# Two token blocks share an accumulator by halves: four 64x64 parts of TensorE in the last loop of an attention and spectral-mixing kernel

## The chip, the cores and the metric

One core of a Trainium2 chip runs the whole program. The metric is the device time of one execution in microseconds (us). A ratio is the mean time of one kernel's fast runs over that of the other's of the same rounds, with a 95% interval; so it is not quite the ratio of the medians that stand beside it. The span of a trace is some 1.8 us shorter than the time. In profile lines PE is TensorE, DVE VectorE, ACT ScalarE, POOL GpSimd and SP SyncE; PSUM is the memory that TensorE's accumulators lie in.

## The reference, cut to what matters

Causal attention over 8 batches, 8 heads and 576 positions gives x (8, 576, 512). The second half mixes it:

```python
def _moe_ref(x, w_r, w_i, w_ch):
    X = np.fft.rfft(x, axis=1)
    ... # 64 modes, each multiplied by its own complex 512x512 matrix
    y = np.fft.irfft(Y, n=S, axis=1)
    u = x + y
    return (u + np.maximum(u @ w_ch, 0.0)).astype(np.float32)
```

576 positions are four full blocks of 128 and one of 64 per batch.

## The kernel before: the parts that matter

The last loop makes the output. A pair is two token blocks, (b, T) and (b, T+1); for the 64-row tails a pair packs four of them. Each pair has two accumulators `us` for u = x + y and two, `zs`, for u @ w_ch. The product x @ w_ch of a pair was made earlier and kept, in one of two ways: as two fp16 digits, which TensorE adds back with four identity matmuls ("e"), or as fp32, which ACT copies into PSUM ("s").

```python
ways = dict(zip(kept, "esesessesesseses"))

def keep_product(i, xx, z):
    if ways[i] != "e":
        nc.scalar.copy(out=z1s[i][:, xx], in_=z)
        return
    nc.scalar.copy(out=z1s[i][:, 0, xx], in_=z)               # high digit
    nc.vector.tensor_tensor(out=z1s[i][:, 1, xx], in0=z,      # low digit
                            in1=z1s[i][:, 0, xx], op=ALU.subtract)

def start_u(i):                      # x into u: one full matmul for each block
    ...
            nc.tensor.matmul(us[i][x][r, :]..., ident, x_all[: r.stop - r.start, :, bb, T, :],
                             start=True, stop=False, ..., tile_position=(0, r.start))

def finish(i):
    for x, (b, T) in enumerate(pairs[i]):
        o = rs[i][:, x, :]
        ...
        nc.vector.tensor_tensor(out=o, in0=us[i][x], in1=o, op=ALU.add)
        for r, bb, _ in parts(b, T):
            nc.sync.dma_start(out=out[bb, bass.ds(T * P, r.stop - r.start), :], in_=rs[i][r, x, :])

for i in range(NPRE, len(pairs)):
    pre(i)                           # digits of z ("e"), then y into z: two matmuls
    start_u(i)
    add_y(us[i], i, 0)               # y into u: two matmuls
    if ways.get(i + 1) == "s":
        seed(i + 1)                  # ACT copy
    ...
    relu(i, 2 if i == last else 1)   # ACT
    finish(i)                        # two additions on DVE, two stores from SyncE
```

Ahead of the loop, a stretch bound by the transfer of weights multiplies the modes and keeps the remaining products (`late`, the pairs not kept during attention), the last pair's last.

The softmax here doesn't subtract the row's maximum and nothing guards it: scores larger than these inputs give would overflow.

## Time and profile before

| what | before |
|---|---|
| median of three runs | 459.39 us |
| last group of weights multiplied, in the trace | 418.11 us |
| last loop on PE | 423.90 to 452.1 us |
| a store of 256 KB: form, time to landing | 128 rows in one run, 2.0 to 4.5 us (medians 2.3 and 2.6) |

### The profile page before, as it was taken

The numbers are of one execution on the slowest core, as the hardware profiler recorded it, in microseconds if no ns is written. First come the engines' busy times: TensorE is split into PE (matmuls) and PEld (weight loads), VectorE is DVE, ScalarE is ACT, GpSimd is POOL, SyncE is SP. The second block draws the span as 40 slices with busy tenths as digits, with TensorE's granted clock in tenths as the row PEclk, the third lists the DMA queues.
The fourth block names the chain that finished last, engine by engine and source line by source line (L and its number), as shares of the span: only waits on it lengthen the run. The fifth ranks groups of instructions, "written<-read, shape, count | busy, mean of one in ns | idle before, by whom it ended". The sixth has DMA issues, their size and how long they took to land.

```text
span 457.1 us, 10262 instructions
## 1 busy us (share of the span) xinstructions
PE 339.1 (74%) x4177; PEld 217.2 (48%) x4209; DVE 237.3 (52%) x528; ACT 219.1 (48%) x382; POOL 182.9 (40%) x269
## 2 busy tenths in 40 slices
PE   1779968966562979936587766779967769797995
PEld 1556646644341656614355544446643326343432
DVE  7777645653242556624345544466656425442675
ACT  1587856554241747723445345446622220221895
POOL 6755555544345555344454444355423223200000
PEclk9999999998586889957778799899999778999999
DMA  9999999999999999999999999999999999995688
GB/s 177 201 203 203 202 201 204 202 204 204 204 204 201 202 202 202 204 205 204 199 192 205 204 204 204 204 203 202 207 206 212 210 210 210 214 214 105 235 285 319
DMA packets 109375, 94.54 MB, mean 207 GB/s; under 512 B 28480, under 2 KB 104512, under 8 KB 109328
## 3 DMA queue, kind: packets, MB, share of 16 engines
q0 software_dynamic: 98960, 81.81, 113.0%
q1 hardware_dynamic: 10368, 12.07, 8.5%
q8 instruction: 33, 0.54, 0.4%
q14 instruction: 14, 0.11, 0.1%
HBM read 164.56 MB, written 9.44 MB: 381 GB/s over the span
## 4 chain that ended last, share of the span: by engine, by line
DMA 70%; PE 20%; issue 4%; POOL 3%; DVE 2%; DVEq 0%; POOLq 0%
DMA w_sb<-in_moe_w_i_dram 44%; DMA q<-in_q_dram 13%; DMA w_sb<-in_moe_w_r_dram 5%; PE yp L441 3%; PE sc_ps L365 3%; PE av_ps L394 2%; DMA x_all<-in_moe_w_r_dram 2%; DMA k<-in_k_dram 2%; PE sc_ps L359 2%; DMA y_acc<-in_moe_w_i_dram 2%; PE tr_ps L324 2%; DMA y_acc<-in_moe_w_r_dram 2%; PE u_ps L694 2%; PE z_ps L675 2%; PE u_ps L675 2%
## 5 line engine op out<-in xcount | busy, mean ns | idle before, releaser
L373 ACT ACTIVATE p_sb<-sc_ps,cumt_sb 128x576 f16<-128x576 f32 (+1 forms) x256 | 141.9, 636 | 45.8 <-PE sc_ps L365 45.4
L217 POOL DMA_DIRECT2D w_sb<-in_moe_w_i_dram x60 | 45.1, 751 | 81.7 <-PE yp L441 36.8
L217 POOL DMA_DIRECT2D w_sb<-in_moe_w_r_dram x60 | 45.4, 757 | 65.2 <-DMA w_sb<-in_moe_w_r_dram 26.1
L217 POOL DMA_DIRECT2D v<-in_v_dram x72 | 50.8, 707 | 31.3 <-DMA w_sb<-in_moe_w_r_dram 8.4
L324 PE MATMUL tr_ps<-ident,q 64*64 64x64 bf16 x576 | 17.1, 208 | 55.4 <-DMA q<-in_q_dram 55.4
L359 PE MATMUL sc_ps<-negm,ident 128*128 128x256 bf16 x256 | 55.0, 300 | 0.3
L441 PE MATMUL yp<-w_sb,xs 128*32 128x512 bf16 x480 | 37.0, 408 | 22.2 <-DMA w_sb<-in_moe_w_i_dram 18.1
L327 DVE COPY qtA<-tr_ps 64x576 bf16<-64x576 bf16 x32 | 23.8, 743 | 50.8 <-PE tr_ps L324 50.7
L344 ACT ACTIVATE p<-sc_ps,cumt 128x64 f16<-128x64 f32 x32 | 10.1, 314 | 74.2 <-PE sc_ps L340 74.2
L394 PE MATMUL av_ps<-v,p_sb 128*128 128x65 f16 x1024 | 43.7, 196 | 0.0
L394 PEld LDWEIGHTS <-p_sb 128*128 128x128 f16 x1024 | 38.9, 99 | 4.8 <-issue 0.7
L327 DVE COPY ktA<-tr_ps 64x576 bf16<-64x576 bf16 x32 | 24.0, 750 | 32.7 <-PE tr_ps L324 32.7
L324 PEld LDWEIGHTS <-q 64*64 64x64 bf16 x576 | 13.3, 120 | 58.0 <-DMA q<-in_q_dram 56.9
L441 PEld LDWEIGHTS <-xs 128*32 128x32 bf16 x512 | 22.9, 169 | 32.3 <-issue 28.8
L365 PE MATMUL sc_ps<-qtB,ktB 128*128 128x64 bf16 (+2 forms) x160 | 34.8, 322 | 3.7 <-issue 2.4
L365 PE MATMUL sc_ps<-qtA,ktA 65*128 65x512 bf16 (+2 forms) x192 | 36.1, 297 | 0.3 <-DVE ktA L327 0.3
L399 DVE TENSOR_REDUCE den<-av_ps 128x5 f32<-128x10 f32 x64 | 10.8, 169 | 46.4 <-PE av_ps L394 46.4
L404 DVE TENSOR_TENSOR x_all<-av_ps,rcp 128x320 f16<-128x320 f32 x64 | 31.5, 492 | 2.2
L327 ACT COPY ktB<-tr_ps 64x576 bf16<-64x576 bf16 x32 | 20.3, 634 | 19.7 <-DVE ktA L327 18.8
L365 PEld LDWEIGHTS <-ktB 128*128 128x128 bf16 x192 | 22.4, 117 | 14.8 <-issue 6.3
L324 PE MATMUL tr_ps<-ident,k 64*64 64x64 bf16 x576 | 17.5, 210 | 14.0 <-DVE qtB L327 10.5
L601 PE MATMUL z_ps<-wch_sb,xs 128*128 128x512 f16 x96 | 26.2, 423 | 0.8 <-DVE xs L595 0.8
(112 smaller groups left out, 526.4 us busy)
## 6 DMA issues: line engine op xcount, KB each, us to landing
w_sb<-in_moe_w_r_dram POOLq DMA_DIRECT2D x60, 512.0 KB, 11.9
w_sb<-in_moe_w_i_dram POOLq DMA_DIRECT2D x60, 512.0 KB, 11.9
q<-in_q_dram POOLq DMA_DIRECT2D x32, 144.0 KB, 9.7
k<-in_k_dram POOLq DMA_DIRECT2D x32, 144.0 KB, 10.1
v<-in_v_dram POOLq DMA_DIRECT2D x72, 64.0 KB, 9.7
out_dram<-r_sb SPq DMA_DIRECT2D x16, 256.0 KB, 2.3
out_dram<-r_w SPq DMA_DIRECT2D x16, 256.0 KB, 2.6
x_all<-in_moe_w_i_dram POOLq DMA_DIRECT2D x3, 512.0 KB, 10.0
```

Of the source, the lines that this page charges most:

```text
L217: nc.gpsimd.dma_start(out=dst, in_=src)
L324: nc.tensor.transpose(ps[rows, r, :], src[rows, r, :], ident16[rows, rows])
L327: copy(out=dst[n % NQ][rows, :].rearrange("d (p r) -> d p r", r=R), in_=ps[rows].rearrange("d r p -> d p r"),)
L359: nc.tensor.matmul(ps[:, bass.ds(w * S, W)], ident16, negm[:, bass.ts(r, W)], start=True, stop=False, skip_group_check=True,)
L365: nc.tensor.matmul(ps[:, c0 : c0 + i1 - i0], keys[:, w, r, :], qt[:, i0:i1], start=False, stop=True, skip_group_check=True,)
L373: nc.scalar.activation(out=pt[:, poff[x] : poff[x] + S - w * W], in_=ps[:, w * S : (w + 1) * S - w * W], func=ACTF.Exp, bias=cumt_sb[:, x, ...
L394: nc.tensor.matmul(ps[:, I, r : r + NCH], lhsT, rhs, start=(i == 0), stop=(i == len(todo) - 1), skip_group_check=True,)
L399: nc.vector.tensor_reduce(out=den, in_=ps[:, :, 0 : VW : NCH], axis=mybir.AxisListType.X, op=ALU.add)
L404: nc.vector.tensor_tensor(out=x_all[:, g, b, :, D * h : D * h + D], in0=ps[:, :, 1 : NCH], in1=rcp.unsqueeze(2).to_broadcast([P, NT, D]), ...
L441: nc.tensor.matmul(ps[32 * cg : 32 * cg + 32, :], cols[:, c0 : c0 + 32, c * MC + 2 * cg + par], wt[(g, c, ri, par)][:, cg, :], start=(x == ...
L601: nc.tensor.matmul(z[:, x, :], xts[i][:, x, dt, :], wch_sb[:, dt, :], start=(dt == 0), stop=(last and dt == DT - 1), skip_group_check=True,)
L675: nc.tensor.matmul(dst[x][r, :], G_sb[rows, bass.ds(T * P, r.stop - r.start)], yv[rows, bb, which, :], start=start, stop=True, skip_group_ ...
```

## The change

Its intent: TensorE is the bound of the last loop, and an identity matmul uses a 128x128 array to move 128 rows. If accumulator h holds half h (64 rows) of both blocks of a pair, four 64x64 parts can bring four quarters in at once. The columns of the constant that brings y in are permuted to match, and for ACT pairs the copies of transposed x are too (not shown). The letters change to twelve digit pairs ("f") and four ACT pairs, and the output rows of an accumulator are now two runs of 64 rows.

```diff
+    two = np.arange(NF * P).reshape(NF // 2, 2, 2, HP).transpose(0, 2, 1, 3).reshape(-1)
+    G_np[:, : NF * P] = G_np[:, two]
-    ways = dict(zip(kept, "esesessesesseses"))
+    ways = dict(zip(kept, "ffsfffffsfsffsff"))
 ...
     def start_u(i):
+        if halved(i):
+            for h in range(2):
+                for x, (b, T) in enumerate(pairs[i]):
+                    own = slice(HP * h, HP * (h + 1))
+                    nc.tensor.matmul(
+                        us[i][h][HP * x : HP * (x + 1), :].rearrange("p (g d) -> p g d", d=P),
+                        ident16h[own, own], x_all[own, :, b, T, :],
+                        start=True, stop=False, ..., tile_position=(HP * h, HP * x),
+                    )
+            return
 ...
     def finish(i):
+            if halved(i):
+                two = out[b, bass.ds((T - x) * P, 2 * P), :]
+                nc.sync.dma_start(out=two.rearrange("(x h p) e -> h x p e", x=2, h=2)[x], in_=o)
+                continue
 ...
-                        zs[i][:, x, :], ident16h, z1s[i][:, y, x, :],     # four full matmuls
+                            zs[i][HP * x : HP * (x + 1), h, :], ident16h[own, own],
+                            z1s[i][own, y, x, :],                        # eight of 64x64
```

## The prediction

> **What bounds the kernel now.** I read four views, in this order. First the page's slices, to see which stage is bound by what: DMA is at nine tenths in every slice until the weights are in, PE at nine only in some. Second the chain of waits, backwards from the end: up to 418.11 us it consists of transfers of weights, and from there to 451.6 us of TensorE work with hardly another engine between. So the last 39 us are a different regime from the rest, and the change sits there. Third a table of four stretches of that ending:
>
> ```profile
> core 0: us, PE busy (x) PEld busy (x) DVE busy (x) ACT busy (x) POOL busy (x), PEclk, DMA share, GB/s
> 396.00:418.00 22.00, 18.46 (x117) 8.61 (x115) 7.67 (x11) 3.20 (x4) 0.74 (x1) 0.92 1.12 198
> 418.00:423.90 5.90, 5.08 (x34) 2.83 (x34) 2.89 (x6) 2.61 (x5) 0.00 (x0) 1.00 0.16 44
> 423.90:452.10 28.20, 28.18 (x137) 11.52 (x135) 20.22 (x32) 24.84 (x27) 0.00 (x0) 1.00 0.84 297
> ```
>
> The third line is the last loop, 16 pairs of token blocks: PE 28.18 of 28.20 us, at full clock, ACT 24.84, DVE 20.22. PE is the bound, ACT is near. Before it (first line) DMA share is 1.12: that stretch waits for weights.
>
> Fourth, the order of time on PE, because what a matmul costs there is the distance of starts, not its busy time:
>
> ```profile
> 426.93 0.59 PE L675 MATMUL u_ps<-yv,G_sb 128*128 128x512 f16 x2
> 427.36 1.03 PE L808 MATMUL z_ps<-r_sb,ident16h 128*128 128x512 f16 x4
> 428.31 0.62 PE L675 MATMUL z_ps<-yv,G_sb 128*64 128x512 f16 x4
> 428.87 0.62 PE L694 MATMUL u_ps<-x_all,ident16h 64*64 64x512 f16 x4
> 429.42 0.62 PE L675 MATMUL u_ps<-yv,G_sb 128*64 128x512 f16 x4
> 429.97 0.60 PE L675 MATMUL z_ps<-yv,G_sb 128*128 128x512 f16 x2
> 430.41 0.59 PE L694 MATMUL u_ps<-x_all,ident16h 128*128 128x512 f16 x2
> 430.85 0.38 PE L675 MATMUL u_ps<-yv,G_sb 128*128 128x512 f16 x1
> ```
>
> This is a pair of the short last blocks, which already works with half-width tiles, between ordinary pairs. 426.93 to 427.36 is two full matmuls: 0.216 us each. The three middle groups of four run two tiles side by side, so each is two passes of 512 columns, 0.432 us; but they follow each other at (429.97 - 428.31)/3 = 0.553. So a narrow group costs some 0.12 us over its passes. Going in, the four full matmuls from 427.36 take 0.95 where 4 x 0.216 = 0.86; coming out, 429.97 to 430.41 is 0.44. I split this as 0.093 for each change of tile shape plus 0.024 for the first step inside a narrow group and 0.010 inside a wide one: 0.117 per narrow group, 0.103 per wide group that follows a narrow one.
>
> **What the Trainium skill says.** "TensorEngine Tiling (Array Packing)", Key Properties: changing the tiling mode, not just the tile, drains TensorE. The trace agrees, 0.093 us a change. The same page, Tiling Modes, gives 64x64 as four independent tiles, and "TensorE: Matmul & The Clock Gate", Part 3, models packed tiles as one matmul's duration plus some 4 ns for each further tile. This trace shows two tiles at once at 64x512 (above) and four at 128*32, but never four of 64x64. The tiling page's Gotcha 1 says that different row tiles may not use one PSUM bank at the same time. The change respects it: half h of the partitions writes accumulator h, a bank of its own. That is what "the same half of two blocks" is for.
>
> **The change part by part.** Let a pass be 512 columns streamed once, 0.216 us.
>
> Loop before: seven pairs bring kept digits in by four full matmuls (two digits, two blocks), nine seed the accumulator by an ACT copy. Every ordinary pair then has two passes for y into z, two for x into u, two for y into u. So six ordinary digit pairs have 10 passes, eight ordinary ACT pairs 6, the two short pairs 10 and 6: 60 + 48 + 16 = 124 passes, 26.78 us. Six narrow groups add 0.70, two returns 0.21: 27.69. Measured is from 423.90 to the last start at 451.71 plus a pass, 28.02. The rest, 0.33, I put down to waits for ACT where two ACT-seeded pairs follow each other.
>
> Loop after: the 16 letters give twelve digit pairs and four ACT pairs, both short pairs among the latter. Digits: eight matmuls of 64x64, four at once, 2 passes instead of 4. x: four at once, 1 pass instead of 2. A digit pair has 2 + 2 + 1 + 2 = 7 passes, an ordinary ACT pair 5, a short pair 6: 84 + 10 + 12 = 106 passes, 22.90 us. But the y matmuls stay full. So a digit pair alternates 64x64, 128x128, 64x64, 128x128: two narrow groups and two returns. Narrow groups: 24 + 2 + 6 = 32, at 0.117 is 3.74. Returns: 24 + 2 = 26, at 0.103 is 2.68. Sum 29.32 us, so the loop gets 1.30 longer: 18 passes saved (3.89) and 0.33 of waits, against 26 more narrow groups (3.04) and 24 more returns (2.47). For one pair: digit pair 10 x 0.216 = 2.16 before, 7 x 0.216 + 2 x 0.117 + 2 x 0.103 = 1.95 after. It is better for like and like by 0.21, but five pairs go from an ACT seed at 1.30 on PE to digits at 1.95. That is where the loss is.
>
> The end: the last pair was ACT-seeded. Its copy (1.02) ran ahead of the relu of the pair before:
>
> ```profile
> 448.91 1.02 ACT L804 COPY z_ps<-z 128x1024 f32<-128x1024 f32 x1
> 449.96 1.02 ACT L713 ACTIVATE r_sb<-z_ps 128x1024 f32<-128x1024 f32 x1
> 451.02 2.48 DVE L728 TENSOR_TENSOR r_sb<-u_ps,r_sb 128x512 f32<-128x512 f32 x4 [0.82 <-ACT r_sb L713]
> 451.49 0.59 PE L675 MATMUL u_ps<-yv,G_sb 128*128 128x512 f16 x2
> ```
>
> DVE's four last additions end at 453.50, 1.80 after PE's last start. Now the last pair brings digits, ACT is free, and DVE waits only for the last accumulators: the first is done 0.15 after PE's last start (0.38 less a pass), then two additions of 0.60 and 0.68 and a small hand-over make 1.46. Gain 0.34.
>
> Ahead of the loop: x for the first two pairs enters by four parts too. For the first pair it lies in a wait for weights; for the second, two passes (0.43) become one plus a narrow group and a return (0.43): nothing. Low digits need a DVE subtraction: four more pairs in the attention stage (8 of about 0.69, 5.5 us) and one more late (1.23). DVE is half idle there and DMA sets the time; nothing. Stores: the same bytes in the same rows. Result permuted in the copies and in the constant: nothing.
>
> Sum: 459.39 + 1.30 - 0.34 = 460.35. I add 0.25 because loading weights into four tiles may cost more than into two: below, 16 matmuls in groups of four take 1.05 where four passes are 0.86, 0.19 over instead of 0.12. Those weights are read with a stride and the change's identity is not, so I take a small part of 26 x 0.07 = 1.8. Predicted 460.6.
>
> ```profile
> 406.52 1.11 PE L441 MATMUL yp<-w_sb,xs 128*32 128x512 bf16 x16
> 407.57 0.62 PE L591 MATMUL xt_ps<-ident16h,x_all 128*128 128x128 f16 x8
> ```
>
> **Rivals.** (1) Only passes count, since the change of shape hides behind streaming. Then the loop has 22.9 us on PE; DVE with 16 x 2 x 0.64 = 20.5 would be close behind. Time 459.39 - 5.1 - 0.34, about 454. For it: somebody chose twelve digit pairs, which pays only if digits are cheap. Against: the three groups above. (2) The four 64x64 parts go two at a time. Then digits take 4 passes and x takes 2, so 3 x 12 + 2 = 38 passes more: +8.2, some 469. For it: no record of four 64x64. Against: four tiles of 128*32 do run together, and the banks differ. (3) ACT was the hidden bound. It goes from 24.8 to some 20, and the 0.33 plus 0.34 above are all that this can give, as PE had 0.02 of 28.20 us idle. (4) DVE's added subtractions delay the release of weight buffers before 418: +0.5 at most, as a whole queue of transfers stands in flight.
>
> **Range and chances.** The switching cost is repeated closely in the trace, so the core is 460 to 461; four-tile loading reaches to 462.2; a hidden part of the switches pulls to 459. Range 458.8 to 462.4. Two per cent is 9.2 us: faster needs more than rival 1, slower needs rival 2 in full and more. Faster 0.02, same 0.95, slower 0.03.
>
> **What would show it.** In the new trace: a digit pair every 1.95 us on PE; 0.31 from the last start of one shape to the first of the next; the four parts starting within some 10 ns; PE still without idle time in the loop, 29.3 us long; ACT near 20 us; DVE's last addition 1.4 to 1.5 us after PE's last start; weights landed at 418 as before. Wrong if a digit pair takes 1.5 (rival 1) or over 2.5 (rival 2), or if the end of the weights moves by over 1 us.

## More of the kernel before

The page of the kernel before: mean busy share of the 16 DMA engines over 40 slices of the span and what they moved, then the queue that SyncE's transfers use (packets, MB, share), then SyncE's stores (count, size, median us from issue to landing).

```profile
DMA  9999999999999999999999999999999999995688
GB/s 177 201 203 203 202 201 204 202 204 204 204 204 201 202 202 202 204 205 204 199 192 205 204 204 204 204 203 202 207 206 212 210 210 210 214 214 105 235 285 319
q1 hardware_dynamic: 10368, 12.07, 8.5%
out_dram<-r_sb SPq DMA_DIRECT2D x16, 256.0 KB, 2.3
out_dram<-r_w SPq DMA_DIRECT2D x16, 256.0 KB, 2.6
```

The last three digits (from 422.8 us) are the last loop: there the stores alone keep DMA at six to eight tenths, at up to 319 GB/s.

## The result, and the profile after

The changed kernel is correct. Its median is 598.40 us (597.34 to 599.19, six runs), beside 459.19 us for the kernel before in the same rounds: ratio 1.3031 (1.3014 to 1.3047). It is 139 us slower, where the prediction's range was 458.8 to 462.4.

The page after, the same lines. It has no time to landing for the stores any more.

```profile
DMA  9999999999999999999999999999111211211111
GB/s 181 201 204 201 202 203 205 204 204 201 200 203 204 204 203 193 204 203 204 205 203 204 207 211 212 209 215 192 41 52 63 71 51 51 84 51 51 51 51 46
q1 hardware_dynamic: 9920, 12.07, 6.5%
out_dram<-r_sb SPq DMA_DIRECT2D x16, 256.0 KB
out_dram<-r_w SPq DMA_DIRECT2D x16, 256.0 KB
```

A slice is now 14.9 us long, for 11.4 before. Up to slice 28, which ends at 417 us, the digits are as before. After it DMA is busy at one or two tenths and moves 41 to 84 GB/s, 51 in half of the slices. The same megabytes cross this queue (12.07), with 448 packets fewer. 448 is 32 x 14, and the kernel makes 32 stores of the new form: each closes with 14 packets fewer than before.

Three stretches of the trace after: before the loop's start, the 7.9 us up to it, and the rest.

```profile
396.00:418.00 22.00, 17.29 (x111) 7.62 (x108) 8.80 (x12) 3.20 (x4) 0.74 (x1) 0.84 1.11 195
418.00:425.86 7.86, 7.14 (x49) 3.30 (x45) 2.93 (x7) 2.65 (x5) 0.00 (x0) 1.00 0.16 45
425.86:596.00 170.14, 40.72 (x233) 8.79 (x232) 21.59 (x34) 19.97 (x21) 0.00 (x0) 0.59 0.16 56
```

The ending takes 170.14 us with PE busy for 40.72 and everything else for less. DMA share is 0.16: of 16 engines that is two and a half. From 545 to 596 us, where the stores are almost all that runs, it is 0.13: two. Who waits for whom from 418 us on (total us, times, longest):

```profile
DVE r_sb L743 <- ACT r_sb L736: 94.0, 9, 18.8
ACT r_sb L736 <- DMA out_dram<-r_sb: 94.0, 7, 19.5
PEld L830 <- issue: 41.8, 14, 15.0
PE z_ps L830 <- ACT r_sb L736: 35.6, 3, 15.0
```

Read it from the second line: the relu on ACT waits 94 us for stores, because it writes into a result buffer that an earlier store is still reading. DVE waits for that ACT, and PE for an accumulator that ACT has not emptied. It is one chain of waits that begins at a store. In the chain that ended last the long pieces are of one kind (start, us, what):

```profile
472.31 18.74 DMA out_dram<-r_sb
...
493.13 18.42 DMA out_dram<-r_sb
...
525.04 18.57 DMA out_dram<-r_sb
```

SyncE issues steadily in such a stretch: 435.37, 440.41, 445.47, 450.50, one store every 5.05 us. 256 KB in 5.05 us is 51.9 GB/s, the page's 51. So the stores go one after the other at the rate of the engines they have, 32 x 5.05 = 161.6 us in all, more than five times the 28 us of the loop that had hidden them.

What the prediction was about can also be read, before the first wait. One digit pair on PE:

```profile
425.86 0.63 PE L830 MATMUL z_ps<-r_sb,ident16h 64*64 64x512 f16 x8
426.42 0.61 PE L688 MATMUL z_ps<-yv,G_sb 128*128 128x512 f16 x2
426.95 0.41 PE L709 MATMUL u_ps<-x_all,ident16h 64*64 64x512 f16 x4
427.30 0.61 PE L688 MATMUL u_ps<-yv,G_sb 128*128 128x512 f16 x2
```

The next pair starts at 427.83: 1.97 us, where 1.95 was predicted. The four parts start at 425.859, 425.863, 425.866 and 425.869, so they do run at once, and the shape changes cost what was read from before.

What the Trainium skill has on it: "DMA: Bandwidth & Descriptors", section "Why a DMA increments its semaphore by 16 and not by 1", says that a transfer runs on the largest number of engines, at most 16, that divides the slowest dimension (not of size 1) of both access patterns, and that of a transfer issued by SyncE only these engines post a completion. The new store's destination is two runs of 64 rows, so its slowest dimension is 2. Two signs of this trace agree: a DMA share of 0.13, two of 16 engines, and 14 packets fewer a store. The page was there to be read before predicting; I did not look it up, because I took the store for unchanged.

### The profile page after: what moved, and what is told of

It is laid out like the page before. It is cut to its first block, busy times and chain, and to the rows that moved or that the text cites. A ratio compares the mean times of both kernels' runs of the same rounds, so it can differ in the third digit from the quotient of the medians.

```text
span 596.1 us, 10499 instructions
## 1 busy us (share of the span) xinstructions
PE 359.9 (60%) x4309; PEld 215.9 (36%) x4309; DVE 243.2 (41%) x537; ACT 213.9 (36%) x377; POOL 182.8 (31%) x269
## 3 DMA queue, kind: packets, MB, share of 16 engines
q1 hardware_dynamic: 9920, 12.07, 6.5%
## 4 chain that ended last, share of the span: by engine, by line
DMA 62%; PE 17%; DVE 6%; issue 3%; ACT 2%; POOL 1%; SPq 0%; DVEq 0%; ACTq 0%; POOLq 0%
DMA w_sb<-in_moe_w_i_dram 23%; DMA out_dram<-r_sb 17%; DMA q<-in_q_dram 10%; DMA w_sb<-in_moe_w_r_dram 9%; PE yp L445 3%; PE sc_ps L369 3%; PE z_ps L614 2%; PE sc_ps L363 2%; PE av_ps L398 2%; PE tr_ps L328 2%; ACT r_sb L736 1%; PE ft_ps L422 1%; PE z_ps L517 1%; DMA xs<-c_negm 1%; DMA qtA<-ncum_sb 1%
## 5 line engine op out<-in xcount | busy, mean ns | idle before, releaser
L743 DVE TENSOR_TENSOR r_sb<-u_ps,r_sb 128x512 f32<-128x512 f32 x20 | 12.9, 686 | 94.8 <-ACT r_sb L736 94.0
L736 ACT ACTIVATE r_sb<-z_ps 128x1024 f32<-128x1024 f32 (+1 forms) x12 | 10.4, 880 | 98.3 <-DMA out_dram<-r_sb 94.0
L369 PE MATMUL sc_ps<-qtB,ktB 128*128 128x512 bf16 (+2 forms) x192 | 44.6, 350 | 0.0
```

What stands on the lines that cost most here:

```text
L369: nc.tensor.matmul(ps[:, c0 : c0 + i1 - i0], keys[:, w, r, :], qt[:, i0:i1], start=False, stop=True, skip_group_check=True,)
L736: nc.scalar.activation(out=rs[i][:, n * x : n * x + n], in_=zs[i][:, n * x : n * x + n], func=ACTF.Relu)
```

## The experiments

Theory A: the form of the store costs it all. Rival B: the 64x64 parts or the switches stall TensorE in a way that the first pairs don't show. A second question was left for the small difference: does the predicted sum of 460.35 us hold once the stores are out of the way?

### Stores as plain rows

```diff
-                two = out[b, bass.ds((T - x) * P, 2 * P), :]
-                nc.sync.dma_start(out=two.rearrange("(x h p) e -> h x p e", x=2, h=2)[x], in_=o)
+                nc.sync.dma_start(out=out[b, bass.ds(T * P, P), :], in_=o)
```

> The changed kernel, but each accumulator's result is stored as one run of 128 rows, as in the kernel before (the result is wrong on purpose: half blocks land in each other's place; bytes, number and size of stores are those of the change). Theory A (the store's form alone costs the 139 us: its slowest dimension is 2, so it runs on 2 of the 16 DMA engines): 460 to 461.5 us, the prediction's sum for the TensorE part, the loop back at 29.3 us and DMA busy again at some 0.8. Theory B (the four 64x64 parts or the change of tile shape stall TensorE): stays above 550.

Measured: 461.38 us (wrong result, as meant), ratio to before 1.0047 (1.0031 to 1.0064). The 139 us are gone; 2.2 us are left. B falls.

### The old kernel with the new store

The destination in the kernel before becomes `two.rearrange("(x h p) e -> h x p e", x=2, h=2)[x]`, and x=4 and x=16 in two sisters; nothing else changes.

> The kernel before with nothing changed but the form of the ordinary stores: two runs of 64 rows, the slowest dimension 2, as in the change (wrong result on purpose). Theory A: 590 to 600 us, 32 stores of 5.05 us one after another. Theory B: 459 to 460.

> The kernel before with stores of four runs of 32 rows, the slowest dimension 4 (wrong result on purpose). Theory A: four engines, 2.5 us a store, 32 x 2.5 = 81 us from 424 on, so 508 to 518 us in all. If a store in several runs is slow whatever the number of engines: 590 or more.

> The kernel before with stores of sixteen runs of 8 rows, the slowest dimension 16 (wrong result on purpose), beside the runs with 2 (597.4 us) and 4 (517.6 us). Theory A: 16 engines again, 459 to 460 us. If every store of several runs were slow: above 480.

Measured: 597.37 us, 517.56 us and 461.35 us. The first is the time of the changed kernel within 0.2%, with none of its matmuls. SyncE's queue on the three pages, in that order:

```profile
q1 hardware_dynamic: 9920, 12.07, 6.4%
```

```profile
q1 hardware_dynamic: 9984, 12.07, 7.8%
```

```profile
q1 hardware_dynamic: 10368, 12.07, 9.1%
```

10368 - 9984 = 384 = 32 x 12, and with sixteen runs the count of before is back: the engines are 2, 4 and 16. The slices of the last loop agree: 51 GB/s in most with two runs, 96 to 133 with four. It is not that several runs are slow; it is how many there are. With sixteen the time is 1.4 us over what I expected: its stores land after 3.2 to 3.3 us by the page, those of before after 2.3 to 2.6, and the last one is on the path to the end. So the order of the rows has a price too, with all 16 engines at work: the first store, with little else in flight, lands after 2.83 us in place of 2.05.

### Three correct stores

The rows can't simply be listed in another order within one transfer: the same skill page says, under "Rules for kernel authors", that an on-chip access pattern takes its partition from its first dimension alone (no run here shows it). What is left is to cut differently.

The first waits for both halves and stores one block from 64 partitions:

```diff
+                if x == 1:
+                    for y, (bb, TT) in enumerate(pairs[i]):
+                        nc.sync.dma_start(
+                            out=out[bb, bass.ds(TT * P, P), :].rearrange("(h p) e -> p h e", h=2),
+                            in_=rs[i][HP * y : HP * (y + 1)])
```

> The changed kernel, correct, but after both additions of a pair one store for each token block: 64 partitions outermost, then the two halves, then the row; still two stores of 256 KB a pair. Theory A: all 16 engines, 460.5 to 462.5 us (some 0.6 more than the plain rows because no store starts after the first addition). Theory B, or if rows that are not one run are slow to write whatever engines take them: far above, 500 and more.

The second makes two stores of 64 rows of each accumulator's result; the third issues every second of them from GpSimd:

```diff
+                for y in range(2):
+                    eng = nc.sync if y == 0 else (nc.scalar if i == len(pairs) - 1 else nc.gpsimd)
+                    eng.dma_start(out=out[b, bass.ds((T - x + y) * P + HP * x, HP), :],
+                                  in_=o[HP * y : HP * (y + 1)])
```

> The changed kernel, correct: each accumulator's store split into two stores of 64 rows, all issued by SyncE. Theory A: each runs on 16 engines; but SyncE then issues 72 stores, some 0.6 us apart by the trace of before, 43 us from 425.4 on: 469 to 473 us, bound by issuing. If issuing is cheaper or is hidden: 461.5 to 462.5.

> The same, correct, with every second store of 64 rows issued by GpSimd (by ACT for the last pair). Theory A with issuing as the next bound: no queue issues over 36, so 461 to 463 us, as the plain rows. If stores from GpSimd land so late that the result buffers come free late: 465 and more.

Measured: 466.60, 478.02 and 464.51 us, all correct, all above what was expected (ratios 1.0154, 1.0402, 1.0103). In the first, a store of 256 KB from 64 partitions takes 3.9 us to land (median), against 2.1 and 2.5 for the two result buffers with plain rows:

```profile
out_dram<-r_sb SPq DMA_DIRECT2D x16, 256.0 KB, 3.9
```

Part of that is crowding: the first store of each run, with little else in flight, takes 3.22 against 2.04. Whether the rest is due to the 64 partitions or to the order of the rows, this run does not separate. In the second, SyncE issues 72 stores from 424.69 to 472.45, 0.67 us apart on average. I had taken 0.6. It is SyncE that sets the end there: PE's last start is at 456.05, close to the 455.45 with plain rows, and each half store lands 2.35 us after its issue (median). In the third no queue is the bound by its count, and two queues put more in flight: the same half stores land 3.4 to 4.0 us after issue (medians). A repair of the form thus brings 598 down to 464.5, and the stores still cost 3 us over plain rows.

### The 2 us that the plain rows leave

The prediction's sum was 460.35; plain rows take 461.38, and in its trace the last loop starts at 426.18 in place of 423.90. First DVE, then PE of the plain-rows run, just before the last weights:

```profile
403.42 1.23 DVE L498 TENSOR_TENSOR z<-z_ps,z 128x1024 f16<-128x1024 f32 x1 [0.77 <-ACT z L497]
404.56 1.28 DVE L603 CAST xs<-xt_ps 128x512 f16<-128x512 f32 x2
```

```profile
402.18 0.61 PE L598 MATMUL xt_ps<-ident16h,x_all 128*128 128x128 f16 x8
405.90 3.60 PE L614 MATMUL z_ps<-wch_sb,xs 128*128 128x512 f16 x8 [3.11 <-DVE xs L603]
409.43 0.68 PE L445 MATMUL yp<-w_sb,xs 128*32 128x512 bf16 x4
```

And PE of the kernel before at the same place:

```profile
403.51 0.61 PE L591 MATMUL xt_ps<-ident16h,x_all 128*128 128x128 f16 x8
404.69 1.90 PE L601 MATMUL z_ps<-wch_sb,xs 128*128 128x512 f16 x8 [0.56 <-DVE xs L595]
406.52 0.47 PE L441 MATMUL yp<-w_sb,xs 128*32 128x512 bf16 x4
```

The last pair now brings digits. The subtraction for its low digit (1.23 us) stands on DVE ahead of the two copies that the first pair's product needs. PE idles 3.11 us, and the eight matmuls after it take 3.60 us where they took 1.90: half the clock. "TensorE: Matmul & The Clock Gate", Part 1, has this: after an idle window of some 3.4 us the clock halves, until PE has been busy for about as long. The trace shows the halving, but after less: the granted clock fell at 405.11, 2.3 us after PE's last matmul ended, and was whole again at 411.93, 6.0 us after PE went on. The last weights had landed by 417.90 and were multiplied at 420.25.

To test it, the product kept last becomes pair 15's, an ACT copy alone:

```diff
     late = [i for i in kept if i not in first_pairs]
+    late.append(late.pop(late.index(15)))
```

> The run with plain rows (461.4 us, wrong result on purpose), and the product kept last before the end is pair 15's, by one ACT copy, in place of pair 17's, whose low digit takes a DVE subtraction besides. Theory C: with the change that subtraction stands on DVE ahead of the two copies that the first pair's product waits for, PE idles 3.1 us, its clock falls to half, and the last weights are multiplied 2.1 us after they landed; then this run is 2 us faster, 459 to 459.7, PE waits for the last weights again, and the last loop still takes 29.5 us. Rival: the low clock there is chance; then 461 to 461.7.

Measured: 460.62 us, ratio 1.0020 (1.0004 to 1.0036), against 1.0047 before. In its trace the last weights are multiplied at 419.03, 0.04 us after they landed: PE waits for them again. The ratios say 1.2 us (their intervals just overlap), and the loop starts 1.24 us earlier in the trace, at 424.94. I had expected 2, from the lag of the last weights (to 420.25, against 418.11 before): so about half came. In this trace the weights themselves landed 1.1 us later; their end moves by a us between traces. The trace has no half clock at this place any more; PE's gap there is 1.16 us. What is left, 1.1 us by the medians and 0.9 by the ratio, agrees with what the prediction had for the TensorE part (0.96), within an interval of 0.2 to 1.7.

The loop of this run on PE takes 424.94 to 454.21 and one pass, 29.49 us, where the prediction had 29.32. DVE ends 1.54 us after PE's last start; predicted 1.46.

### Sharing one stretch of 64x64 tiles

If the switches eat the gain, halving their number should bring it. The kept digits of the next pair are moved to stand right after x of this pair:

```diff
         start_u(i)
+        if ways.get(i + 1) == "f":
+            seed(i + 1)
         add_y(us[i], i, 0)
```

First with plain rows, so that stores play no part:

> The merged order (kept digits of the next pair enter together with x of this one) with the stores as plain rows (wrong result on purpose), so that stores play no part: against the 460.6 us of the same kernel without merging it isolates the switches. By the prediction's terms 12 narrow groups (0.117) and 12 returns (0.103) fewer, 2.6 us: loop 26.9 to 27.2 us on PE in place of 29.5, time 457.9 to 458.5. If switches are hidden: 460.6.

Measured: 459.07 us, ratio 1.0000 (0.9981 to 1.0020). The loops of the two runs, in order without and with sharing:

```profile
424.90:454.60 29.70, 29.69 (x233) 7.49 (x232) 20.75 (x33) 20.06 (x21) 0.00 (x0) 1.00 0.81 285
```

```profile
424.30:451.70 27.40, 27.40 (x233) 8.56 (x232) 20.64 (x33) 20.00 (x22) 0.00 (x0) 1.00 0.84 297
```

PE gains 2.3 us, with the same matmuls in number and size. Counted properly, 11 narrow groups and 9 returns fell away, 11 x 0.117 + 9 x 0.103 = 2.2 us; I had written twelve of each. But the time fell by 1.5 us only by the medians, and by 0.9 by the ratios, whose intervals overlap. The last store was issued at 452.91 in place of 455.78, 2.9 us earlier (0.6 of it from an earlier start of the loop), and landed 3.20 us later in place of 2.04: with PE faster, the stores run into one another.

Then correct, with the split stores, the subtraction moved and the sharing:

> As the run before, correct, with pair 15's product kept last, and the kept digits of the next pair enter right after x of this pair, so that both share one stretch of 64x64 tiles: one change to narrow and one back a pair in place of two. By the prediction's terms a digit pair falls from 1.95 to 7 x 0.216 + 0.117 + 0.103 = 1.73 us and the loop from 29.5 to some 26.9: 456 to 457.5 us, faster than the kernel before by 0.5%. If the switches are not what costs: 459 to 460.

Measured: 462.63 us, a miss by 5 us. PE is done as early as expected, last start 451.71, but the last relu waits for a result buffer:

```profile
ACT r_sb L737 <- DMA out_dram<-r_sb: 3.9, 1, 3.9
```

So the last pair was given the deeper ring of buffers, and the short pairs' stores were divided too. Then came one ACT pair more (pairs 14 and 16 in place of 15, and pair 16's product kept last). The edit of the ring:

```diff
-        if i % 2 == 0 or i == len(pairs) - 1:
+        if i % 2 == 0:
```

> Correct. The merged kernel with split stores, whose trace has PE finished as early as expected (451.7) but the last relu waiting 3.9 us for its result buffer until a store of an earlier pair has landed. Here the last pair's result goes to the other, deeper ring, and the short pairs' stores alternate between SyncE and GpSimd. If that wait is what ate the gain: 459 to 460 us, and no wait of ACT for a store. If the stores themselves (64 partitions each, DMA at 0.86) set the end: 461 to 462.5.

> Correct. As the run before, with one more pair seeded by ACT in place of digits (five instead of four): two passes fewer on PE, 0.43 us, and 1.02 more on ACT. PE sets the end: 0.4 us under the run before, 458.6 to 459.6. Stores or ACT set it: no gain.

Measured: 461.00 and 460.96 us, both correct, ratios 1.0034 (1.0015 to 1.0052) and 1.0036 (1.0020 to 1.0052). The wait is gone, and of it 1.6 us came, for both edits together; the ACT pair brought nothing. The stores set the end now. In the first of the two, PE's last start is at 451.12 and DVE ends at 452.67, both earlier than in the kernel before (451.71 and 453.50), yet the last store lands at 458.59 in place of 455.83:

```profile
out_dram<-r_w SPq DMA_DIRECT2D x18, 128.0 KB, 3.8
out_dram<-r_w POOLq DMA_DIRECT2D x16, 128.0 KB, 3.7
```

Half a block takes longer to land here than a whole one did before. That is crowding in the main: issued by SyncE alone, above, the same half block landed after 2.35 us, and the first of this run after 2.41. No correct version with halved accumulators beat the kernel before; the best is 0.3% slower. Whether a layout exists that has both four parts at once and stores of 128 rows in one run stays open.

## Why the prediction was wrong

- The step that failed is the sentence "Stores: the same bytes in the same rows." Bytes and rows are the same; the number of engines is not. The prediction put that term at nothing, and it measured 137 us: 598.4 against 461.4 with plain rows, and 597.4 when the old kernel gets the new store. None of the four rivals contained it. The third was about ACT and the fourth about DVE; neither asked what the new store looks like to the DMA.
- A second, small step failed: "DVE is half idle there and DMA sets the time; nothing." The share of busy time was right. But the subtraction stood in the queue right ahead of copies that PE waited for, and an idle PE lost half its clock. It cost 1.2 us by the ratios, with a wide interval. Rival 4 saw the right engine and the wrong consequence, a late release of weight buffers; the weights landed as before.
- The TensorE account held. A digit pair took 1.97 us for 1.95, the loop 29.49 us for 29.32, the end gained 0.26 for 0.34, the four parts ran at once (rival 2 falls), and the switches are not hidden (rival 1 falls, and sharing a stretch took out 2.3 us for some 2.2 by the terms). The extra 0.25 for loading four tiles was hardly needed. One term stays unproven: 0.33 us of the loop before were put down to waits for ACT, and the loop after has 0.17 over its sum as well.
- "ACT was the hidden bound" (rival 3): ACT went from 24.84 to some 20 us, as expected, and gave no more than its share.

## What to carry to other kernels

When a change regroups rows of a result, follow them to the store and write out its access pattern as the instruction carries it: here an outermost dimension of 2 took away 14 of 16 DMA engines. A hidden transfer has a rate at which it stops being hidden; here stores at 51.9 GB/s, for some 297 in the loop before, turned a loop bound by PE into one bound by stores, and the sign was one eighth of DMA with PE busy for 41 of 170 us. Small tiles pay more when their groups stand together, since each change of tile shape cost some 0.1 us, half of a 512-column pass: sharing a stretch took 2.3 us off the loop on PE. Even so the time only came level with the kernel before (ratio 1.0000), and with the wrong result.

## What the Trainium skill lacked or had wrong

- "DMA: Bandwidth & Descriptors" had the rule for the number of engines, and the runs confirm it for 2, 4 and 16 (597.4, 517.6 and 461.4 us; 14, 12 and 0 completion packets fewer a store). What it lacks is the price of stores that do use all 16 engines but not 128 partitions with rows in order. With little else in flight, 256 KB from 128 partitions in order landed after 2.04 us; from 128 partitions in sixteen runs after 2.83; from 64 partitions, two rows each, after 3.22; and 128 KB from 64 partitions after 2.3.
- The same page has no interval measured on this chip at which SyncE can issue stores one after the other: 0.67 us here on average, over 72 stores of 128 KB, though some of 256 KB in the kernel before are only 0.46 to 0.50 apart.
- "TensorEngine Tiling (Array Packing)" says that changing the mode drains TensorE, without a figure: 0.093 us a change here, and 0.117 or 0.103 with the slower first step of the new shape. Its speedups leave this out: bringing x in by four parts, alone between full matmuls, gains nothing by these terms (one pass and 0.22 us against two passes of 0.216).
- "TensorE: Matmul & The Clock Gate", Part 1, puts the idle time that halves the clock at a window of some 3.4 us. Here the clock fell 2.3 us into a gap of 3.11 us, after which eight matmuls took 3.60 us in place of 1.90.
